# Masked attention taken through TensorE a unit of three steps at a time, with float32 scores

## The chip, the cores and the metric

One core of a Trainium2 chip. The metric is the device time of one execution in microseconds, as the median of several runs. The profile is of one execution on the same core.

## What is computed

Attention with a linear distance penalty, over 2 batches, 8 heads, 768 positions and 64 columns a head, then two feed-forward layers on 1536 tokens of 512 columns with 2048 hidden columns. A query sees the first 8 keys and its last 96 (both numbers are inputs):

```python
scores = scale * np.matmul(q, k.transpose(0, 1, 3, 2))
keep = is_global | is_local
scores = np.where(keep, scores + bias, -1000000000.0)
a = np.exp(scores - np.max(scores, axis=-1, keepdims=True))
a = a / (np.sum(a, axis=-1, keepdims=True) + 1e-09)
x = np.matmul(a, v)                       # then reshaped to (1536, 512)
h = x @ w_in;  x = (h / (1 + np.exp(-h))) @ w_out
h = x @ w_in2; out = (h * np.clip(h + 3, 0, 6) / 6) @ w_out2
```

q and k are float32 with values of about 0.66 in size; the weights come as float64 and are decoded on the chip.

## The kernel before, in words

**Units and steps.** The attention is cut into 16 units: a batch, a half of 384 positions, and a pair of heads. In the code they are counted from 0 with the pair running fastest, then the half, then the batch; units 0 to 3 and 8 to 11 have half 0. A unit has HB = 3 steps of 128 queries, so there are 48 steps. For a step, each of the two heads needs 256 keys: 128 of its own block and 128 made of 96 earlier ones and 32 global ones. The first step of a half 0 has 128 keys only.

**Stages of a step** (functions of these names, lines 321 to 440). `stage_a` brings a unit's keys and queries into transposed form: three TensorE transposes of keys and one of the earlier or global ones (psA), three of queries; ACT copies the result as a rounded high part (kh, qh, type float32r), DVE makes the remainder (kl, ql). `stage_b` makes scores as qh·kh + qh·kl + ql·kh, for both heads side by side in the 64-row halves of the array (psS, L388), then DVE adds the penalty and takes the extreme value (L394), then ACT takes the exponential and sums it (L398). `stage_b2` makes reciprocals of the sums on DVE (L404, L405) and scales z on POOL (L407). `stage_c` turns z by TensorE (psT, L416) and copies it out (pt: ACT for the first step of a unit, DVE for the others). `stage_d` multiplies with the values (psO, L435), both heads side by side in the 64-column halves of the array; after a unit's third step ACT copies the result as high part (xh, L439) and DVE makes the remainder (xl, L440).

**Order.** `attention_loop(n)` writes step n's scores, step n-1's scaling, step n-3's turn and step n-4's value products; `transposes(n)` adds a key part or a query part every third step each. `loop(n)` puts around it one piece of the feed-forward stage from `todo`, and the pieces of decoding weights and of gates from `late` and `slots`. The first pieces of the feed-forward layer are spread among the attention: from n = PRE = 16 one at every second step, 18 of them; after step 52 one at every step. An H piece is 12 matmuls (psH, L510), a Y piece 6 (psY, L683); in this first part of the stream they have 384 columns. During the attention all of them go through one PSUM bank, "f". Engines TensorE, ACT and POOL run in program order through the attention (`manual_schedule`); DVE and the SP queue are ordered by a scheduler at build time. At the start, before the loop, all are in program order.

**PSUM.** Eight banks in four rings: "S" 2 for scores (with "f" taking turns in the first 15 steps), "tr" 3 for transposes of any kind, "o" 2 for value products, "f" 1.

Of the kernel before, what the change touches and what calls it, by code (L numbers as in the profile page):

```python
# [18 lines left out]
P = 128  # L19
# [9 lines left out]
def attention_ffn_kernel(ctx, tc, q, k, v, n_global, n_local, w_in1, w_out1, w_in2, w_out2, out):  # L29
# [30 lines left out]
    ps_bufs = {"S": 2, "tr": 3, "o": 2, "f": 1}  # L60
# [136 lines left out]
    CL = 3  # L197
    LAG = CL + 1
    KOFF, QOFF, APOS, ATAG = 4, 3, 2, "tr"
    PRE = 3 * NP + LAG  # L200

# [17 lines left out]
    ZB = 4  # L219
# [42 lines left out]
    t1 = apool.tile([P, 2, W], F32, name="pat1", tag="z", bufs=ZB)  # L262
    t2 = apool.tile([P, 2, W], F32, name="pat2", tag="z", bufs=ZB)
# [57 lines left out]
    def stage_a(u, part):  # L321

        b, half, p = units[u]
        rk, kp, rq, rv, vp = raw[u]
        if part == 0:
            tr[u] = tuple(apool.tile([P, w], F32R, name=f"{n}{u}", tag=n) for n, w in (("kh", KW), ("kl", KW), ("qh", TB), ("ql", TB)))
        kh, kl, qh, ql = tr[u]
        ps = bank(ATAG, f"psA{u}_{part}")
# [26 lines left out]

        def glo(x):
            return x.unsqueeze(1).to_broadcast([P, HB - 1, G])


        parts = [(lambda x: tiles(x)[:, :, :P], own(ps[:, :TB])), (lambda x: tiles(x)[:, :HB - 1, P:], glo(ps[:, m - G:m]))]  # L360
        if half:
            parts.append((lambda x: x[:, :P], ps[:, TB:m]))

        def evac():
            for at_, src in parts:
                nc.scalar.copy(at_(kh), src)

        def rest():
            for at_, src in parts:
                nc.vector.tensor_tensor(out=at_(kl), in0=src, in1=at_(kh).bitcast(F32), op=ALU.subtract)  # L370

        return evac, rest

    zt, smt, ptt, pso = {}, {}, {}, {}

    def first(u, t):
        return units[u][1] == 0 and t == 0

    def stage_b(n, u, t):
        b, half, p = units[u]  # L380
        kh, kl, qh, ql = tr[u]
        tags = ("SS", "fS", "Sf")[n % 3] if n < PRE - 1 else "SS"
        ps = [bank(tags[h], f"psS{u}_{t}_{h}") for h in range(2)]
        o = P if first(u, t) else t * SP
        for i, (a, c) in enumerate(((qh, kh), (qh, kl), (ql, kh))):
            for h in range(2):
                hs = slice(h * D, (h + 1) * D)
                nc.tensor.matmul(ps[h][:, :W], a[hs, t * P:(t + 1) * P], c[hs, o:o + W], start=i == 0, stop=i == 2)  # L388
        w, nb = (P, nbs[p][0]) if first(u, t) else (W, nbs[p][1])
        z = apool.tile([P, 2, W], F32, name=f"z{u}_{t}", tag="z", bufs=ZB)  # L390
        mn = apool.tile([P, 2], F32, name=f"mn{u}_{t}", tag="mn", bufs=3)
        sm = apool.tile([P, 2], F32, name=f"sm{u}_{t}", tag="sm", bufs=3)
        for h in range(2):
            nc.vector.tensor_tensor_reduce(  # L394
                out=z[:, h, :w], in0=ps[h][:, :w], in1=nb[:, h, :], scale=1.0, scalar=3e38,
                op0=ALU.add, op1=ALU.min, accum_out=mn[:, h:h + 1])
        for h in range(2):
            nc.scalar.activation(out=z[:, h, :w], in_=z[:, h, :w], func=AF.Exp, bias=mn[:, h:h + 1], scale=-1.0,  # L398
                                 accum_out=sm[:, h:h + 1])
        zt[u, t], smt[u, t] = z, sm  # L400

    def stage_b2(u, t):
        z, sm, w = zt[u, t], smt.pop((u, t)), P if first(u, t) else W
        nc.vector.tensor_scalar(out=sm, in0=sm, scalar1=1e-9, scalar2=None, op0=ALU.add)  # L404
        nc.vector.reciprocal(sm, sm)  # L405
        for h in range(2):
            nc.gpsimd.tensor_scalar(out=z[:, h, :w], in0=z[:, h, :w], scalar1=sm[:, h:h + 1], scalar2=1.0,  # L407
                                    op0=ALU.mult, op1=ALU.mult)

    def stage_c(u, t):  # L410
        z = zt.pop((u, t))
        n = 1 if first(u, t) else 2
        ps = bank("tr", f"psT{u}_{t}").rearrange("p (h c q) -> p h c q", h=2, c=2)
        for h in range(2):
            for c in range(n):
                nc.tensor.transpose(ps[:, h, c, :], z[:, h, c * P:(c + 1) * P], ident)  # L416
        pt = apool.tile([P, 2, 2, P], F32, name=f"pt{u}_{t}", tag="pt")
        if t:
            nc.vector.tensor_copy(pt[:, :, :n, :], ps[:, :, :n, :])
        else:  # L420
            nc.scalar.copy(pt[:, :, :n, :], ps[:, :, :n, :])
        ptt[u, t] = pt

    def stage_d(u, t):
        b, half, p = units[u]
        rk, kp, rq, rv, vp = raw[u]
        pt = ptt.pop((u, t))
        if t == 0:
            pso[0] = bank("o", f"psO{u}")
        ps = pso[0]  # L430
        n = 1 if first(u, t) else 2
        for c in range(n):
            for h in range(2):
                lhs = (rv if c == n - 1 else vp)[:, h, t, :]
                nc.tensor.matmul(ps[h * D:(h + 1) * D, t * P:(t + 1) * P], lhs, pt[:, h, c, :], start=c == 0, stop=c == n - 1)  # L435
        if t == HB - 1:
            i = 2 * b + half
            hi, lo = (x[:, p, i * TB:(i + 1) * TB] for x in (xh, xl))
            nc.scalar.copy(hi, ps[:, :TB])  # L439
            return lambda: nc.vector.tensor_tensor(out=lo, in0=ps[:, :TB], in1=hi.bitcast(F32), op=ALU.subtract)  # L440

    seq = [(u, t) for u in range(len(units)) for t in range(HB)]
# [5 lines left out]
    def attention_loop(n):  # L448
        for f in queue.pop(n, []):
            f()  # L450
        if n < len(seq):
            u, t = seq[n]
            stage_b(n, u, t)
            if t == HB - 1 and u + 1 < NP:
                biases(u + 1)
        if n == 0:
            e, r = stage_a(1, 0)
            e()
            r()
            beyond()  # L460
        if 0 <= n - 1 < len(seq):
            stage_b2(*seq[n - 1])
        for f in rests.pop(n, []):
            f()
        if APOS == 0:
            transposes(n)
        if 0 <= n - CL < len(seq):
            stage_c(*seq[n - CL])
        if 0 <= n - LAG < len(seq):
            u, t = seq[n - LAG]  # L470
            f = stage_d(u, t)
            if f:
                at(n + 1, f)
                if u + 2 < len(units):
                    loads_v(u + 2)

        if APOS == 1:
            transposes(n)

    def transposes(n):  # L480
        for d, part in ((KOFF, 0), (QOFF, 1)):
            if (n + d) % HB == 0 and 1 <= (n + d) // HB < len(units):
                e, r = stage_a((n + d) // HB, part)
                e()
                rests.setdefault(n + 1, []).append(r)
                if part and (n + d) // HB + 2 < len(units):
                    loads((n + d) // HB + 2)

# [5 lines left out]
    def ffn_bank(kind, name):  # L494
        tags = ({"h": ("f",), "y": ("f",)}, {"h": ("f", "S"), "y": ("tr", "o")}, {"h": ("S",), "y": ("f", "o")})[ready[0]]
        ring = [t for t in tags[kind] if t in ps_bufs for _ in range(ps_bufs[t])]
# [265 lines left out]
    with tc.manual_schedule(engines=None):  # L762
        nc.vector.memset(three, 3.0)
        for i, ap in enumerate((n_global, n_local)):
# [21 lines left out]
    def loop(n):  # L786
# [5 lines left out]
        if APOS == 2:  # L792
            transposes(n)
# [271 lines left out]
```

## Time and profile before

| | us |
|---|---|
| median of 3 runs | 642.38 (640.3 to 645.43) |
| profiled execution, first to last instruction (span) | 638.6 |
| TensorE busy in the span | 617.2 |
| DVE / ACT / POOL busy | 489.9 / 417.4 / 161.0 |

The span is what the profile covers; the time of a run includes what lies before the first and after the last instruction. A second number of the profiled execution's own time is not in the profile, so the span stands for it. An engine's busy time counts stretches in which at least one of its instructions runs; matmuls overlap in the rows, so a row's duration is longer than its share of the engine.

### The profile page before, as it was taken

To read this page: it belongs to the slowest core of one execution; us is meant where nothing else is said; L and a number is where in the kernel's file an instruction comes from. 1 tells how busy PE (TensorE), PEld (TensorE's weight loads), DVE (VectorE), ACT (ScalarE), POOL (GpSimd) and SP (SyncE) were. 2 spreads that over 40 slices of the span, in tenths; PEclk is the share of its full clock that TensorE was granted. 3 is DMA by queue.
4 is the path that set the end of the run, shared out by engine and by line. 5 is a ranking of instruction groups with operands and counts; after the bars stand their busy time and mean duration, and the time that the engine had idled before them with its cause. 6 is when DMAs were issued, how large, how long until landed. Compare 5 with 4: busy or idle time off the path is not lost.

```text
span 638.6 us, 9729 instructions
## 1 busy us (share of the span) xinstructions
PE 617.2 (97%) x3214; PEld 498.9 (78%) x3214; DVE 489.9 (77%) x1107; ACT 417.4 (65%) x887; POOL 161.0 (25%) x233
## 2 busy tenths in 40 slices
PE   5889999999999999999999998999999999999996
PEld 3667777789888788888888887887788888888885
DVE  5899889953578796767675679988979696969453
ACT  4787877765557576666666676765766666666760
POOL 2776666561111111111212120011111111111110
PEclk9999999999999999999999999999999999999999
DMA  6555645349577667777776793186576868686544
GB/s 174 136 139 136 149 112 137 99 150 204 103 162 166 144 146 176 161 180 166 181 163 134 164 198 100 66 247 150 132 173 165 182 157 181 157 176 162 100 102 166
DMA packets 81625, 97.31 MB, mean 152 GB/s; under 512 B 55456, under 2 KB 55456, under 8 KB 81312
## 3 DMA queue, kind: packets, MB, share of 16 engines
q0 software_dynamic: 12576, 45.09, 37.7%
q1 hardware_dynamic: 68992, 51.53, 26.8%
q8 instruction: 27, 0.44, 0.3%
q14 instruction: 30, 0.25, 0.1%
HBM read 46.27 MB, written 3.15 MB: 77 GB/s over the span
## 4 chain that ended last, share of the span: by engine, by line
PE 35%; issue 25%; POOL 5%; DVE 2%; DMA 2%; ACT 1%; POOLq 0%; ACTq 0%; SPq 0%; DVEq 0%
PE psY L683 19%; PE psH L510 9%; POOL y L712 5%; PE psP_b L591 3%; PE psP_c L591 2%; PE psP_a L591 2%; DMA y<-st 1%; DMA raw<-in_moe_w_in_dram 1%; ACT st L708 0%; DVE g L541 0%; DVE da L1027 0%; DVE wol L148 0%; DVE dc L134 0%; DVE u L608 0%; ACT da L103 0%
## 5 line engine op out<-in xcount | busy, mean ns | idle before, releaser
L712 POOL DMA_DIRECT2D y<-st x78 | 66.9, 857 | 362.4 <-ACT st L708 357.2
L708 ACT COPY st<-psY 128x512 f32<-128x512 f32 x156 | 91.3, 586 | 51.6 <-PE psY L683 47.5
L510 PE MATMUL psH<-xh,wih 128*128 128x512 f32 (+1 forms) x216 | 83.2, 385 | 1.7 <-DVE g L541 1.7
L510 PE MATMUL psH<-xl,wih 128*128 128x512 f32 (+1 forms) x216 | 82.5, 382 | 0.0
L510 PE MATMUL psH<-xh,wil 128*128 128x512 f32 (+1 forms) x216 | 82.4, 382 | 0.0
L683 PE MATMUL psY<-gh,woh 128*128 128x512 f32 (+1 forms) x160 | 61.4, 384 | 0.0
L683 PE MATMUL psY<-gh,wol 128*128 128x512 f32 (+1 forms) x160 | 60.6, 378 | 0.0
L683 PE MATMUL psY<-gl,woh 128*128 128x512 f32 (+1 forms) x160 | 60.5, 378 | 0.0
L398 ACT ACTIVATE z<-z,mn 128x256 f32<-128x256 f32 (+1 forms) x96 | 46.5, 486 | 21.1 <-DVE mn L394 15.6
L407 POOL TENSOR_SCALAR z<-z,sm 128x256 f32<-128x256 f32 (+1 forms) x96 | 48.2, 514 | 43.9 <-DVE sm L405 18.4
L683 PE MATMUL psY<-woh,gl 128*128 128x512 f32 x144 | 56.1, 390 | 0.1
L683 PE MATMUL psY<-woh,gh 128*128 128x512 f32 x144 | 56.1, 390 | 0.1
L683 PE MATMUL psY<-wol,gh 128*128 128x512 f32 x144 | 56.0, 389 | 0.0
L510 PEld LDWEIGHTS psH<-xh,wih 128*128 128x128 f32 x216 | 40.5, 188 | 10.6 <-DVE g L541 2.1
L103 ACT ACTIVATE da<-raw 128x512 f32<-128x512 f32 x64 | 42.9, 670 | 5.9 <-DMA raw<-in_moe_w_in_dram 5.5
L510 PEld LDWEIGHTS psH<-xl,wih 128*128 128x128 f32 x216 | 40.5, 188 | 7.5 <-DVE xl L620 0.4
L510 PEld LDWEIGHTS psH<-xh,wil 128*128 128x128 f32 x216 | 40.5, 188 | 7.1
L1027 DVE SCALAR_TENSOR_TENSOR da<-raw,da 128x512 int32<-128x512 int32 x64 | 44.3, 693 | 1.2 <-DVE sm L404 0.2
L608 DVE TENSOR_TENSOR u<-psP_c,u 128x512 f32<-128x512 f32 x22 | 15.1, 688 | 34.5 <-ACT u L602 34.5
L532 ACT ACTIVATE a<-psH 128x512 f32<-128x512 f32 (+1 forms) x24 | 14.2, 590 | 40.4 <-PE psH L510 40.3
L551 DVE SCALAR_TENSOR_TENSOR gl<-a,gh 128x512 fp32r<-128x512 f32 (+1 forms) x34 | 23.2, 682 | 21.9 <-ACT gh L545 21.6
L1015 DVE TENSOR_SCALAR da<-da 128x512 f32<-128x512 f32 x64 | 28.3, 442 | 14.7 <-ACT da L103 14.7
(185 smaller groups left out, 1565.2 us busy)
## 6 DMA issues: line engine op xcount, KB each, us to landing
y<-st POOLq DMA_DIRECT2D x78, 512.0 KB, 4.8
raw<-in_moe_w_in_dram SPq DMA_DIRECT2D x32, 512.0 KB, 4.1
raw<-in_moe_w_out_dram SPq DMA_DIRECT2D x32, 512.0 KB, 3.3
rk<-in_k_dram SPq DMA_DIRECT2D x32, 96.0 KB, 2.5
rq<-in_q_dram SPq DMA_DIRECT2D x32, 96.0 KB, 2.9
rv<-in_v_dram SPq DMA_DIRECT2D x32, 96.0 KB, 2.6
out_dram<-y SPq DMA_DIRECT2D x12, 256.0 KB, 2.0
xf<-xh SPq DMA_DIRECT2D x2, 1024.0 KB, 6.7
```

Of the source, the lines that this page charges most:

```text
L103: nc.scalar.activation(out=t["a"], in_=raws[n][:, :, 1].bitcast(F32), func=AF.Abs)
L398: nc.scalar.activation(out=z[:, h, :w], in_=z[:, h, :w], func=AF.Exp, bias=mn[:, h:h + 1], scale=-1.0, accum_out=sm[:, h:h + 1])
L407: nc.gpsimd.tensor_scalar(out=z[:, h, :w], in0=z[:, h, :w], scalar1=sm[:, h:h + 1], scalar2=1.0, op0=ALU.mult, op1=ALU.mult)
L510: nc.tensor.matmul(ps, a[:, kt, js], x[:, kt, n0:n1], start=n == 0, stop=n == 3 * KT - 1)
L551: nc.vector.scalar_tensor_tensor(out=gl[:, j, :], in0=t["a"], scalar=2.0, in1=gh[:, j, :].bitcast(F32), op0=ALU.mult, op1=ALU.subtract)
L591: nc.tensor.matmul(ps, a[:, 2 * k + q, f * P:(f + 1) * P], x, start=p in (1, 5) and n == 0, stop=n == 5, skip_group_check=True)
L608: nc.vector.tensor_tensor(out=u, in0=st["c"], in1=u, op=ALU.add)
L683: nc.tensor.matmul(ps[:, :rhs.shape[1]], lhs, rhs, start=n == 0, stop=n == 3 * FC - 1)
L708: nc.scalar.copy(st[:, m % 2, :], part)
L712: late.setdefault(n, []).append(lambda: nc.gpsimd.dma_start(y, st, accum_op=ALU.add))
L1015: nc.vector.tensor_scalar(out=a, in0=a, scalar1=as_float(897 << 20), scalar2=as_float((1151 << 20) - 1), op0=ALU.max, op1=ALU.min)
L1027: nc.vector.scalar_tensor_tensor(out=ai, in0=w1, scalar=-0x40000000, in1=ai, op0=ALU.bitwise_and, op1=ALU.bitwise_or)
```

## The change

A unit goes through TensorE as a whole. `scores(u)` makes all three steps' scores at n = 3u with one float32 product per head and step, of unsplit queries and keys (kt, qt), into four banks: the two "S" banks hold steps 0 and 1 side by side, the two "o" banks hold step 2. The value products of unit u-2 follow at once, into a "tr" bank. The exponentials stay one step at a time. The sums of unit u-1 are turned into reciprocals once, at n = 3u, and all its z scaled then; its z is turned at n = 3u + 2, three blocks in a row. Key and query parts of unit u+1 stand at n = 3u and 3u + 1. `kl` and `ql` go away; DVE copies the global and earlier keys instead. z is held for two whole units (ZB = 2 of three steps each), pt in three buffers; ACT copies the middle step's pt, DVE the others. PRE becomes 17. Three products of zeros are put ahead of everything on TensorE. The rings of the feed-forward stage keep the same banks, the Y ring in another order.

```diff
-    KOFF, QOFF, APOS, ATAG = 4, 3, 2, "tr"
-    PRE = 3 * NP + LAG
+    LAG = 4
+    PRE = 3 * NP + LAG + 1
...
-    ZB = 4
+    ZB = 2
...
         if part == 0:
-            tr[u] = tuple(apool.tile([P, w], F32R, name=f"{n}{u}", tag=n) for n, w in (("kh", KW), ("kl", KW), ("qh", TB), ("ql", TB)))
+            tr[u] = tuple(apool.tile([P, w], F32, name=f"{n}{u}", tag=n) for n, w in (("kt", KW), ("qt", TB)))
...
         if part:
+            nc.scalar.mul(qt, ps[:, :TB], -1.0 / (D ** 0.5))
+            return
...
+        nc.scalar.copy(tiles(kt)[:, :, :P], own(ps[:, :TB]))
+        nc.vector.tensor_copy(tiles(kt)[:, :HB - 1, P:], glo(ps[:, m - G:m]))
         if half:
+            nc.vector.tensor_copy(kt[:, :P], ps[:, TB:m])
...
+    def scores(u):
+
+        kt, qt = tr[u]
+        two, one = ([bank(tag, f"psS{u}_{tag}{h}") for h in range(2)] for tag in "So")
+        place = {(h, t): one[h][:, :W] if t == 2 else two[h][:, t * W:(t + 1) * W] for h in range(2) for t in range(HB)}
+        for t in range(HB):
+            for h in range(2):
+                hs = slice(h * D, (h + 1) * D)
+                o = P if width(u, t) == P else t * SP
+                nc.tensor.matmul(place[h, t], qt[hs, t * P:(t + 1) * P], kt[hs, o:o + W], start=True, stop=True)
...
+    def normalise(u):
+        z, sm = zt[u], smt[u].rearrange("p t h -> p (t h)")
         nc.vector.tensor_scalar(out=sm, in0=sm, scalar1=1e-9, scalar2=None, op0=ALU.add)
         nc.vector.reciprocal(sm, sm)
+        for t in range(HB):
+            w = width(u, t)
+            for h in range(2):
+                nc.gpsimd.tensor_scalar(out=z[:, t, h, :w], in0=z[:, t, h, :w], scalar1=smt[u][:, t, h:h + 1], scalar2=1.0,
+                                        op0=ALU.mult, op1=ALU.mult)
+
+    def turn(u):
+        z = zt.pop(u)
+        for t in range(HB):
+            n = width(u, t) // P
+            ps = bank("tr", f"psT{u}_{t}").rearrange("p (h c q) -> p h c q", h=2, c=2)
+            for h in range(2):
+                for c in range(n):
+                    nc.tensor.transpose(ps[:, h, c, :], z[:, t, h, c * P:(c + 1) * P], ident)
+            pt = apool.tile([P, 2, 2, P], F32, name=f"pt{u}_{t}", tag="pt", bufs=3)
+            if t == 1:
+                nc.scalar.copy(pt[:, :, :n, :], ps[:, :, :n, :])
+            else:
+                nc.vector.tensor_copy(pt[:, :, :n, :], ps[:, :, :n, :])
+            ptt[u, t] = pt
+
+    def values(u):
...
+        ps = bank("tr", f"psO{u}")
...
+        nc.scalar.copy(hi, ps[:, :TB])
+        return lambda: nc.vector.tensor_tensor(out=lo, in0=ps[:, :TB], in1=hi.bitcast(F32), op=ALU.subtract)
...
     def attention_loop(n):
+        u, t = divmod(n, HB)
         for f in queue.pop(n, []):
             f()
+        if t == 0 and u < len(units):
+            scores(u)
+        if t == 0 and 0 <= u - 2 < len(units):
+            at(n + 1, values(u - 2))
+            if u < len(units):
+                loads_v(u)
+        if u < len(units):
+            exponentials(u, t)
             if t == HB - 1 and u + 1 < NP:
                 biases(u + 1)
         if n == 0:
             beyond()
+        if t == 0 and 0 <= u - 1 < len(units):
+            normalise(u - 1)
         for f in rests.pop(n, []):
             f()
+        if t < 2 and u + 1 < len(units):
+            stage_a(u + 1, t)
+            if t and u + 3 < len(units):
+                loads(u + 3)
+
+    def turns(n):
+        u, t = divmod(n, HB)
+        if t == 2 and 0 <= u - 1 < len(units):
+            turn(u - 1)
...
         nc.vector.memset(three, 3.0)
+        warm = fpool.tile([P, 512], F32, name="warm", tag="a")
+        nc.vector.memset(warm, 0.0)
+        for _ in range(3):
+            nc.tensor.matmul(bank("f", "psW"), warm[:, :P], warm, start=True, stop=True)
```

`exponentials(u, t)` holds the DVE and ACT instructions of `stage_b` unchanged for one step. In `loop(n)`, `turns(n)` stands after the feed-forward piece, where `transposes(n)` stood.

## Rows read from the trace of the kernel before

**Rows 1.** The page: span, and TensorE's busy time with its share.

```profile
span 638.6 us, 9729 instructions
...
PE 617.2 (97%) x3214; PEld 498.9 (78%) x3214; DVE 489.9 (77%) x1107; ACT 417.4 (65%) x887; POOL 161.0 (25%) x233
```

**Rows 2.** Busy us of each engine by stretch: PE, PEld, DVE, ACT, POOL, granted clock, DMA.

```profile
8.00:24.00 16.00, 13.85 (x78) 9.47 (x80) 11.71 (x52) 9.52 (x35) 7.39 (x19) 1.00 0.78 204
24.00:45.00 21.00, 17.91 (x165) 12.38 (x165) 20.13 (x77) 16.77 (x57) 16.36 (x27) 1.00 0.54 129
45.00:126.00 81.00, 79.50 (x678) 59.81 (x677) 74.37 (x272) 63.31 (x209) 53.49 (x80) 1.00 0.52 129
...
141.00:600.00 459.00, 456.00 (x2021) 377.68 (x2021) 352.63 (x628) 300.42 (x531) 69.39 (x80) 1.00 0.70 161
```

**Rows 3.** TensorE's timeline inside one unit: start, us, line, operands, count.

```profile
104.63 0.49 PE L331 MATMUL psA<-ident,rq 128*128 128x128 f32 x3
105.05 0.39 PE L388 MATMUL psS<-kh,qh 64*128 64x256 f32 x2
105.27 0.28 PE L388 MATMUL psS<-kl,qh 64*128 64x256 f32 x2
105.39 0.28 PE L388 MATMUL psS<-kh,ql 64*128 64x256 f32 x2
105.60 0.66 PE L416 MATMUL psT<-ident,z 128*128 128x128 f32 x4
106.18 0.44 PE L435 MATMUL psO<-pt,rv 128*64 128x128 f32 x4
...
107.70 0.44 PE L435 MATMUL psO<-pt,vp 128*64 128x128 f32 x4
...
108.28 0.45 PE L683 MATMUL psY<-gh,woh 128*128 128x384 f32 x1
108.57 0.34 PE L683 MATMUL psY<-gl,woh 128*128 128x384 f32 x1
108.74 0.33 PE L683 MATMUL psY<-gh,wol 128*128 128x384 f32 x1
```

**Rows 4.** Groups by line, 0 to 141 us: count, busy us, mean ns, idle before.

```profile
L407 POOL TENSOR_SCALAR z<-z,sm 128x256 f32<-128x256 f32 (+1 forms) x96 | 48.2, 514 | 43.9 <-DVE sm L405 18.4 <-ACT z L398 8.6 <-ACT kh L366 5.8
...
L419 DVE COPY pt<-psT 128x512 f32<-128x512 f32 x32 | 21.7, 678 | 0.8 <-PE psT L416 0.8
...
L404 DVE TENSOR_SCALAR sm<-sm 128x2 f32<-128x2 f32 x48 | 16.0, 333 | 3.8 <-ACT z L398 3.3
...
L370 DVE TENSOR_TENSOR kl<-psA,kh 128x384 fp32r<-128x384 f32 (+2 forms) x40 | 12.8, 359 | 0.7 <-ACT kh L366 0.7
...
L103 ACT ACTIVATE da<-raw 128x512 f32<-128x512 f32 x8 | 5.4, 679 | 0.0
```

**Rows 5.** ACT's timeline: two exponentials, and xh before the next copy.

```profile
103.31 0.52 ACT L398 ACTIVATE z<-z,mn 128x256 f32<-128x256 f32 x1
...
103.82 0.51 ACT L398 ACTIVATE z<-z,mn 128x256 f32<-128x256 f32 x1
...
104.56 0.49 ACT L439 CAST xh<-psO 128x384 fp32r<-128x384 f32 x1
104.93 0.50 ACT L697 COPY y<-psY 128x384 f32<-128x384 f32 x1
```

**Rows 6.** TensorE's timeline: first scores of units 0, 2, 15; first dense H piece.

```profile
8.09 0.58 PE L388 MATMUL psS<-kh,qh 64*128 64x256 f32 x2 [0.58 <-ACT qh L337]
...
23.86 0.39 PE L388 MATMUL psS<-kh,qh 64*128 64x256 f32 x2
...
126.49 0.39 PE L388 MATMUL psS<-kh,qh 64*128 64x256 f32 x2
...
140.78 0.44 PE L510 MATMUL psH<-xh,wih 128*128 128x384 f32 x1
```

**Rows 7.** TensorE's timeline at the start: the first three key turns.

```profile
5.56 0.87 PE L331 MATMUL psA<-ident,rk 128*128 128x128 f32 x3 [5.56 <-DMA rk<-in_k_dram]
```

More of the change, by code (lines that the diff above doesn't have):

```diff
@@ L368, in rest @@
[L368 to L385, printed above, removed]
+            nc.vector.tensor_copy(kt[:, :P], ps[:, TB:m])
@@ L386, in stage_b, with width @@
+    zt, mnt, smt, ptt, scored = {}, {}, {}, {}, {}
+    def width(u, t):
+        return P if units[u][1] == 0 and t == 0 else W
+    def scores(u):
+        kt, qt = tr[u]
+        two, one = ([bank(tag, f"psS{u}_{tag}{h}") for h in range(2)] for tag in "So")
+        place = {(h, t): one[h][:, :W] if t == 2 else two[h][:, t * W:(t + 1) * W] for h in range(2) for t in range(HB)}
+        for t in range(HB):
             for h in range(2):
                 hs = slice(h * D, (h + 1) * D)
-                nc.tensor.matmul(ps[h][:, :W], a[hs, t * P:(t + 1) * P], c[hs, o:o + W], start=i == 0, stop=i == 2)
@@ L389, in stage_b @@
[L389 to L392, printed above, removed]
+                o = P if width(u, t) == P else t * SP
+                nc.tensor.matmul(place[h, t], qt[hs, t * P:(t + 1) * P], kt[hs, o:o + W], start=True, stop=True)
+        scored[u] = place
+        zt[u] = apool.tile([P, HB, 2, W], F32, name=f"z{u}", tag="z", bufs=ZB)
@@ L397, in stage_b @@
         for h in range(2):
[L398 to L403, printed above, removed]
+            nc.scalar.activation(out=z[:, t, h, :w], in_=z[:, t, h, :w], func=AF.Exp, bias=mn[:, t, h:h + 1], scale=-1.0,
+                                 accum_out=sm[:, t, h:h + 1])
@@ L404, in stage_b2 @@
+    def normalise(u):
+        z, sm = zt[u], smt[u].rearrange("p t h -> p (t h)")
         nc.vector.tensor_scalar(out=sm, in0=sm, scalar1=1e-9, scalar2=None, op0=ALU.add)
         nc.vector.reciprocal(sm, sm)
[L406 to L422, printed above, removed]
@@ L425, in stage_d @@
+    def values(u):
         b, half, p = units[u]
         rk, kp, rq, rv, vp = raw[u]
[L427 to L440, printed above, removed]
@@ L442, in attention_ffn_kernel @@
-    seq = [(u, t) for u in range(len(units)) for t in range(HB)]
+        ps = bank("tr", f"psO{u}")
+        for t in range(HB):
+            pt = ptt.pop((u, t))
+            n = width(u, t) // P
+            for c in range(n):
+                for h in range(2):
+                    lhs = (rv if c == n - 1 else vp)[:, h, t, :]
+                    nc.tensor.matmul(ps[h * D:(h + 1) * D, t * P:(t + 1) * P], lhs, pt[:, h, c, :], start=c == 0, stop=c == n - 1)
+        i = 2 * b + half
+        hi, lo = (x[:, p, i * TB:(i + 1) * TB] for x in (xh, xl))
@@ L494, in ffn_bank @@
     def ffn_bank(kind, name):
[L495 to L496 removed]
+        ring = ({"h": ("f",), "y": ("f",)}, {"h": ("f", "S", "S"), "y": ("tr", "o", "tr", "o", "tr")}, {"h": ("S",), "y": ("f", "o", "o")})[ready[0]][kind]
         tag = ring[rot[kind] % len(ring)]
```

78 lines of the change are left out of this document (17 added, 61 removed).

## The prediction

> **What bounds the kernel now.** I read the page's first part, then the busy time by stretch, then TensorE's own timeline, then the groups by line. TensorE is busy for 617 of 638.6 us [rows 1]. By stretch [rows 2] there are three regimes: from 8 to 24 us it is busy 13.9 of 16; from 24 to 45 DVE is the full engine (20.1 of 21, TensorE 17.9); from 45 on TensorE is (79.5 of 81, then 456 of 459). So a microsecond taken from TensorE's attention work after 45 us should come off the end, if nothing else steps in, and after the attention nothing changes: the feed-forward stage takes the same products at TensorE's pace.
>
> What TensorE does in one attention step stands in [rows 3]. Split scores: three pairs of products (both heads at once, 0.12 us apart) take 0.55 us from 105.05 to 105.60, though 3 x 0.12 is 0.36. Four turns of z: 0.58. Value products, both column blocks: 0.58 (107.70 to 108.28). The feed-forward product after them shows why these sums are round: its first matmul takes 0.29 us to the next, the later ones 0.17. [...] I take 0.15 per change. Then a 128-column turn is (0.58 - 0.15)/4 = 0.108 us. A float32 value product has two records per head (x4 for two heads and one block), also 0.108 each, heads side by side.
>
> **The change, part by part.** Count units from 0 to 15; a unit whose half is 0 lacks a block in its first step.
>
> *TensorE.* Scores of a unit before: 3 x 0.55 = 1.66 us. After: one float32 product per step and head, two records of 256 columns, 2 x 0.108 = 0.215 each; if heads run side by side as both neighbours in [rows 3] do, 3 x 2 x 0.215 + 0.15 = 1.44. If not, 2.7. I take 1.44, since split scores in the same 64-row form and float32 value products both pair. Values: 3 x 0.58 = 1.74 becomes 6 x 0.215 + 0.15 = 1.44 (1.22 for half 0). Turns: 1.74 becomes 12 x 0.108 + 0.1 = 1.4 (1.2). Key and query turns keep their 0.11 each, 0.85 together. So attention costs TensorE about 5.1 us a unit (4.8 for half 0) against 6.1 (5.7): some 1 us, nearly all from fewer changes of form. The float32 pass itself costs more than the three split ones (0.43 against 0.36). If TensorE alone set the pace this were 16 us.
>
> *The others.* DVE loses kl (12.8 us) and ql and two thirds of the sums (16.0 us for 48 now) [rows 4], and gains small copies. That is worth time only between 24 and 45 us, and only until the next limit. POOL keeps its 96 scalings of 0.51 [rows 4]. ACT keeps its exponentials, loses 24 small key casts and gains larger z copies: about even.
>
> *The new wait.* What is late next is the order on ACT. At a unit's first step the program puts scores(u), then values(u-2) with their ACT copy xh, and only then the exponentials of u. ACT runs in that order, so it stands until TensorE has done scores and values: xh starts 1.44 + 1.44 + 0.1 = 3.0 us after scores(u) start. Queued behind it: two exponentials, the copy of kt, two exponentials, the copy of qt. Exponentials go at 0.51 us [rows 5], xh, kt and qt, all casts or copies of 384 columns, 0.37 apart as xh and its follower, with 0.5 until the last has landed [rows 5]: 0.37 + 1.02 + 0.36 + 1.02 + 0.5 = 3.3, so qt(u+1) is there at 6.3. Scores(u+1) need it. Before them in TensorE's order stands the third turn of u-1, which in a ring of three "tr" banks gets the bank of the query turn just copied: 0.1 + 0.43 + 0.1 more, 6.9 us from scores to scores (6.7 or 6.5 where halves 0 are involved). Without that bank it is 6.4. This exceeds TensorE's 5.1 wherever little feed-forward work falls. ACT work put into a first step lies on it too: decode pieces (0.68 long, some 0.6 apart) [rows 4], and gate casts and y copies of 384 columns (0.4 each, as xh).
>
> *Unit by unit.* A feed-forward piece stands at every odd step from 17: H pieces 12 x 0.175 = 2.1 us, Y pieces 6 x 0.175 + 0.1 = 1.15. The larger of TensorE's sum and the ACT loop:
> Units 2 to 4: 6.5 + 0.6, 6.5, 6.7 + 0.6 = 20.9.
> Units 5 to 9: 7.0 (TensorE, an H), 6.9 + 0.4 + 0.6, 7.2 (TensorE), 6.7 + 0.4, 6.7 + 0.6 = 36.5.
> Units 10 to 14: 6.9, 8.1 (TensorE, Y and H), 7.1, 8.2 (TensorE), 7.3 = 37.6.
> In all 95.0. Before, units 2 to 14 lasted from 23.86 to 126.49, 102.6 [rows 6]. Gain 7.6.
>
> *The first two units.* Scores of unit 0 start at 8.1 now and of unit 2 at 23.9 [rows 6]. [...] The three zero products of 512 columns, twice 0.43 us each by the record's pace above, last 2.6 us at full pace and 5.2 at half, from about 1.4 us: they lie beside the wait for data, and at half pace delay the key turns by at most 0.9. The new copy of the global keys stands ahead of the patterns on DVE and may push those from 4.7 to 7 us, so the first exponentials start near 10.4, as now. Units 0 and 1 have no values(u-2) to wait for. From 10.4: exponentials 0.8, key copy and decode 1.0, exponentials 1.0, query copy 0.5 put scores of unit 1 near 13.8; decode 0.6, exponentials 1.0, sums 0.4, six scalings 3.0 and the last turn 0.6 put unit 2 near 19.4. Gain 4.5; between 3 (half pace throughout) and 6 (patterns not held up).
>
> *The tail.* Before, unit 15 to the first dense H piece is 126.49 to 140.78, 14.3 [rows 6]. After, one more Y piece falls behind it: scores 1.44, the values of three units 4.3, the turns of two 2.8, an H piece 2.1, three Y pieces 3.5 make 14.2 of work; the last turns wait for exponentials and six scalings in a burst, and the last values for a z copy of 0.68 [rows 4]: 2 us. So 16.2. Loss 1.9.
>
> **Sum.** 7.6 + 4.5 - 1.9 = 10.2. The span of 638.6 becomes 628.4; the median of the runs, 642.4, lies 3.8 above the span, and that stays: 632.
>
> [...] TensorE still runs at half pace at 8.1 us (a pair of scores takes 0.58) and at full pace at 23.9 (0.39) [rows 6], though between them it is busy 13.9 of 16 us [rows 2]. [...]
>
> **Rivals.**
> 1. Heads not side by side in float32 scores. For: no 64-row float32 product in this trace. Against: both neighbours pair. Price: 1.3 us on the loop and on TensorE in each of 14 units, 1.3 in the tail: +20, 652. It decides from the point where scores of a unit exceed about 2.2 us (10 us over 14 units).
> 2. The clock falls back or never rises early. Unit 2 comes 1.5 us later and two to three units pay 1.44 + 1.1 more: +6, 638.
> 3. More waits in the loop: in-order DVE puts z copies (0.68) ahead of the reductions, or POOL's decode delays scalings. At 7.9 us a unit, the pace of before, units 2 to 14 give nothing: 640.
> 4. The query bank doesn't hold up the third turn: 0.55 less in nine loops, 627; with the loop gone and only TensorE's and ACT's own sums left (5.6 us a unit without feed-forward work, 84 for units 2 to 14) 622.
>
> **How the numbers follow.** Forecast 0.52 (626 to 638), rival 1 0.11, rivals 2 and 3 0.27, rival 4 0.10. One per cent, 6.4 us, is about what a measurement of this kernel can tell from none (its runs spread by 5). Faster than 636: most of the forecast and rival 4, 0.56; within: 0.33; slower: 0.11. The range 623 to 645 leaves out rival 1 and the extremes.
>
> **What would show it.** Right: scores of a unit take about 1.4 us in pairs; ACT idles before xh, released by psO, about 1 us a unit; TensorE idles before psT or psS released by ACT; unit 2 near 19.5, dense H pieces from about 130.5; from there the same length to the end. Wrong: score records one after another (rival 1); turns of 0.21 us after 10 us (2); TensorE without gaps from 45 us on (4); or a longer dense stage, which nothing here foresees.

## The result, and the profile after

| | before | after |
|---|---|---|
| median of the runs | 641.57 us (640.30 to 645.43, 4 runs) | 635.21 us (634.44 to 637.77, 4 runs) |
| after / before | | 0.990, 95% interval 0.987 to 0.993 |
| span of the profiled execution | 638.6 us | 632.8 us |

The changed kernel is 1% faster: 6.4 us by the medians, 5.8 by the spans. A second measurement gave 637.33 against 641.71, ratio 0.992 (0.989 to 0.994). The forecast was 632.0, with 10.2 us of gain in the span. The profiled run of the changed kernel took 634.86 us, 2.1 above its span.

The page of the changed kernel, lines that answer to [rows 1], with the granted clock in 40 slices:

```profile
span 632.8 us, 9365 instructions
...
PE 606.6 (96%) x3124; PEld 496.4 (78%) x3124; DVE 464.5 (73%) x1012; ACT 412.9 (65%) x863; POOL 160.4 (25%) x233
...
PEclk9998999999999999999999999999999999999998
```

TensorE is busy 10.6 us less, DVE 25 us less. The zeros are 5 us of TensorE's new time, but taking them out brings it down by only 1.2, to 605.4 (run 4): the first products then last longer, 24 of them from 4 to 12 us at 5.94 us of busy time, where 26 from 6.42 to 11 us take 3.84 behind the zeros. So on equal footing, without zeros in either kernel, TensorE saves 11.8 us and not the 16 that the prediction gave for TensorE alone. Of the 10.6 us, 5.8 came off the span; TensorE's idle time rose from 21.4 to 26.2. The 8 in the fourth slice is a loss of the clock that the kernel before didn't have. Busy time by stretch, the same windows as [rows 2]:

```profile
8.00:24.00 16.00, 12.01 (x86) 8.37 (x87) 12.82 (x63) 9.91 (x35) 8.41 (x21) 0.89 0.86 215
24.00:45.00 21.00, 15.98 (x149) 11.90 (x149) 17.62 (x65) 16.67 (x55) 14.45 (x25) 1.00 0.55 135
...
45.00:126.00 81.00, 74.25 (x629) 61.32 (x627) 58.17 (x218) 61.97 (x199) 56.32 (x86) 0.98 0.54 129
141.00:600.00 459.00, 456.26 (x2015) 377.01 (x2014) 353.32 (x629) 301.16 (x531) 66.25 (x78) 1.00 0.70 158
```

The dense stage is as it was (456.3 of 459 against 456.0). DVE is no longer the full engine from 24 to 45 us (17.6 of 21 against 20.1). From 45 to 126 us TensorE, full before at 79.5 of 81, now idles 6.75 us. Where the stages begin, from TensorE's timeline, answering to [rows 6, 7]:

```profile
1.50 5.08 PE L739 MATMUL psW<-warm 128*128 128x512 f32 x6 [1.50 <-DVE warm L737]
6.42 0.49 PE L329 MATMUL psA<-ident,rk 128*128 128x128 f32 x3
...
8.14 1.13 PE L369 MATMUL psS_S<-kt,qt 64*128 64x256 f32 x8 [0.58 <-DVE nval L278]
...
14.64 1.58 PE L369 MATMUL psS_S<-kt,qt 64*128 64x256 f32 x8 [3.81 <-ACT qt L331]
...
20.42 0.92 PE L369 MATMUL psS_S<-kt,qt 64*128 64x256 f32 x6
...
119.80 1.13 PE L369 MATMUL psS_S<-kt,qt 64*128 64x256 f32 x8
...
136.34 0.45 PE L482 MATMUL psH<-xh,wih 128*128 128x384 f32 x1
...
143.58 0.39 PE L482 MATMUL psH<-xh,wih 128*128 128x512 f32 x1
```

The last line is the first H piece of 512 columns. In the kernel before it is

```profile
149.23 0.39 PE L510 MATMUL psH<-xh,wih 128*128 128x512 f32 x1
```

So the parts that the prediction gave compare as follows:

| part | before | predicted | after | gain predicted | gain measured |
|---|---|---|---|---|---|
| scores of unit 2 start | 23.86 | 19.4 | 20.42 | 4.5 | 3.4 |
| units 2 to 14 | 102.6 | 95.0 | 99.4 | 7.6 | 3.2 |
| unit 15 to the first dense H piece | 14.3 | 16.2 | 16.5 | -1.9 | -2.2 |
| from there to the end | 497.9 | unchanged | 496.4 | 0 | 1.4 |

Most of the last row is work that changed sides. From the first dense H piece to the first H piece of 512 columns are 8.45 us before and 7.24 after: 24 products psY stand there before, 17 after. At 0.173 us from one to the next the seven make up the 1.21 us. They now stand ahead of the first dense H piece. Up to the first H piece of 512 columns both kernels have done 72 products psY, and from there to the end take 489.4 and 489.2 us.

The lengths of units 2 to 14, from first score to first score, against the prediction's:

| unit | 2 | 3 | 4 | 5 | 6 | 7 | 8 | 9 | 10 | 11 | 12 | 13 | 14 |
|---|---|---|---|---|---|---|---|---|---|---|---|---|---|
| predicted | 7.1 | 6.5 | 7.3 | 7.0 | 7.9 | 7.2 | 7.1 | 7.3 | 6.9 | 8.1 | 7.1 | 8.2 | 7.3 |
| after | 6.96 | 7.17 | 6.67 | **11.69** | 7.29 | 7.60 | 6.53 | 8.31 | 6.38 | 8.51 | 6.52 | 8.89 | 6.85 |

Twelve of the thirteen add up to 87.7 us against 88.0 predicted; there are misses of 0.4 to 1.0 either way in eleven of them, so that their sum agrees is in part luck. Unit 5 alone is 4.7 too long. TensorE's timeline there:

```profile
46.40 0.34 PE L482 MATMUL psH<-xl,wih 128*128 128x384 f32 x1
49.07 0.50 PE L482 MATMUL psH<-xh,wil 128*128 128x384 f32 x1 [2.34 <-POOL wil L148]
49.37 0.52 PE L482 MATMUL psH<-xh,wih 128*128 128x384 f32 x1
...
50.33 2.65 PE L403 MATMUL psT<-ident,z 128*128 128x128 f32 x12
52.91 0.92 PE L369 MATMUL psS_S<-kt,qt 64*128 64x256 f32 x6
```

and the instructions on ACT and POOL that bear on it:

```profile
43.09 0.64 ACT L145 CAST wih<-dc 128x512 fp32r<-128x512 f32 x1
...
45.03 2.76 POOL L393 TENSOR_SCALAR z<-z,sm 128x256 f32<-128x256 f32 x6 [3.93 <-PE psA L336]
47.75 1.27 POOL L148 TENSOR_TENSOR wil<-dc,wih 128x512 fp32r<-128x512 f32 x1
```

The H piece of step 17 is the first to use the second piece of decoded weights, and stops in the middle for its remainder `wil`. Dated from PRE, `wil` falls on step 15, where the program puts the six scalings of unit 4 ahead of it; in the kernel before it fell on step 14. POOL makes it only after them, and stood idle for 3.93 us before them, though the high part `wih` that the remainder is taken from was done at 43.73. Then a second cost: after the 2.34 us of waiting TensorE goes on at half pace (0.32 us from matmul to matmul instead of 0.17, twelve turns in 2.58 instead of 1.4 us); the records of the granted clock give half of the full level, 0.50, from 49.3 to 52.7 us.

Most of the rest behaves as foreseen. Unit 10 on TensorE:

```profile
82.64 1.13 PE L369 MATMUL psS_S<-kt,qt 64*128 64x256 f32 x8
83.61 0.60 PE L369 MATMUL psS_o<-kt,qt 64*128 64x256 f32 x4
84.14 0.44 PE L421 MATMUL psO<-pt,rv 128*64 128x128 f32 x4
...
85.38 0.55 PE L329 MATMUL psA<-ident,rk 128*128 128x128 f32 x3
...
88.47 0.63 PE L403 MATMUL psT<-ident,z 128*128 128x128 f32 x4 [0.17 <-DVE pt L408]
89.02 1.14 PE L369 MATMUL psS_S<-kt,qt 64*128 64x256 f32 x8
```

Twelve score records take 1.50 us (82.64 to 84.14): both heads side by side. On ACT, answering to [rows 5]:

```profile
85.50 0.48 ACT L424 CAST xh<-psO 128x384 fp32r<-128x384 f32 x1 [2.54 <-PE psO L421]
...
88.42 0.47 ACT L331 ACTIVATE qt<-psA 128x384 f32<-128x384 f32 x1
```

ACT stands before xh until the values are done; scores of unit 11 follow 0.13 us after the end of qt (88.89). That fits the predicted loop. The third turn (88.47), though, waits for DVE's pt and runs beside qt, not behind it; it ends when the scores start, so these rows alone don't say which of the two held them. Run 2 tests the order on ACT. The waits from 20 to 137 us, engine, instruction, releaser, total, times, longest:

```profile
ACT xh L424 <- PE psO L421: 24.6, 16, 3.1
...
POOL z L393 <- DVE sm L389: 16.2, 11, 3.9
...
PE psH L482 <- POOL wil L148: 2.3, 1, 2.3
```

And the groups that answer to [rows 4], up to 137 us:

```profile
L393 POOL TENSOR_SCALAR z<-z,sm 128x256 f32<-128x256 f32 (+1 forms) x96 | 45.9, 501 | 26.8 <-DVE sm L389 20.3 <-PE psA L336 3.9 <-PE psO L421 2.6
...
L388 DVE TENSOR_SCALAR sm<-sm 128x6 f32<-128x6 f32 x16 | 5.3, 328 | 0.6 <-ACT z L383 0.6
L351 DVE COPY kt<-psA 128x64 f32<-128x64 f32 x16 | 3.5, 219 | 8.8 <-ACT kt L350 8.8
```

The first instruction on the sums (L388) costs 5.3 us instead of 16.0, and 12.8 us of kl became 3.5 of this copy (and 2.2 of another one).

### The profile page after: what moved, and what is told of

Read it like the earlier page. It is cut to its first block, busy times and chain, and to the rows that moved or that the text cites. A ratio compares the mean times of both kernels' runs of the same rounds, so it can differ in the third digit from the quotient of the medians.

```text
span 632.8 us, 9365 instructions
## 1 busy us (share of the span) xinstructions
PE 606.6 (96%) x3124; PEld 496.4 (78%) x3124; DVE 464.5 (73%) x1012; ACT 412.9 (65%) x863; POOL 160.4 (25%) x233
## 4 chain that ended last, share of the span: by engine, by line
PE 58%; issue 23%; POOL 6%; DVE 5%; ACT 5%; DMA 2%; POOLq 0%; DVEq 0%; SPq 0%; ACTq 0%
PE psY L655 25%; PE psH L482 15%; POOL y L684 4%; PE psP_b L563 3%; PE psO L421 3%; PE psT L403 2%; PE psP_c L563 2%; PE psP_a L563 2%; PE psS_S L369 2%; ACT z L383 2%; DMA y<-st 1%; POOL z L393 1%; PE psW L739 1%; PE psS_o L369 1%; DVE z L379 1%
## 5 line engine op out<-in xcount | busy, mean ns | idle before, releaser
L684 POOL DMA_DIRECT2D y<-st x78 | 66.9, 857 | 364.3 <-ACT st L680 359.1
L393 POOL TENSOR_SCALAR z<-z,sm 128x256 f32<-128x256 f32 (+1 forms) x96 | 45.9, 501 | 26.8 <-DVE sm L389 20.3
L482 PEld LDWEIGHTS psH<-xh,wih 128*128 128x128 f32 x216 | 40.6, 188 | 10.6 <-DVE g L513 1.9
L986 DVE TENSOR_SCALAR da<-da 128x512 f32<-128x512 f32 x64 | 29.5, 461 | 15.9 <-ACT da L103 15.6
L523 DVE SCALAR_TENSOR_TENSOR gl<-a,gh 128x512 fp32r<-128x512 f32 (+1 forms) x34 | 23.1, 681 | 22.4 <-ACT gh L517 22.1
```

Of the source, the lines that this page charges most:

```text
L393: nc.gpsimd.tensor_scalar(out=z[:, t, h, :w], in0=z[:, t, h, :w], scalar1=smt[u][:, t, h:h + 1], scalar2=1.0, op0=ALU.mult, op1=ALU.mult)
L482: nc.tensor.matmul(ps, a[:, kt, js], x[:, kt, n0:n1], start=n == 0, stop=n == 3 * KT - 1)
L523: nc.vector.scalar_tensor_tensor(out=gl[:, j, :], in0=t["a"], scalar=2.0, in1=gh[:, j, :].bitcast(F32), op0=ALU.mult, op1=ALU.subtract)
L684: late.setdefault(n, []).append(lambda: nc.gpsimd.dma_start(y, st, accum_op=ALU.add))
L986: nc.vector.tensor_scalar(out=a, in0=a, scalar1=as_float(897 << 20), scalar2=as_float((1151 << 20) - 1), op0=ALU.max, op1=ALU.min)
```

## The experiments

Twelve kernels ran. The first four shared their runs of the kernel before (median 643.35), the next four too (641.7), and the last four (641.71).

**1. The decoding of that piece one step earlier** (12 steps ahead of step 17, so from step 5 as in the kernel before):

```diff
-        ahead = ((PRE, 11, 5, -1), (33, 27, 21, 15))[i][j] if i < 2 else (17, 13, 9, 5)[j] if chunks[i] == (1, 1) else ((20, 15, 11, 6), (18, 14, 9, 2))[fast(*chunks[i])][j]
+        ahead = ((PRE, 12, 5, -1), (33, 27, 21, 15))[i][j] if i < 2 else (17, 13, 9, 5)[j] if chunks[i] == (1, 1) else ((20, 15, 11, 6), (18, 14, 9, 2))[fast(*chunks[i])][j]
```

> The changed kernel with the second weight piece decoded one step earlier (its slots start at step 5 as before the change, not 6). Theory A (the 11.7 us of unit 5 come from the first H piece, which waits for wil on POOL behind the six scalings of unit 4, and from the half-rate clock that the gap brings): wil is made before that burst, unit 5 takes 7.0 to 7.5 us, no clock drop near 49 us, and the time falls by 4 us below the changed kernel's 635.2, to 631. Rival (the H piece waits anyway, for its values or for the burst itself): unit 5 stays at 10 us or more and the time within 1 us of 635.

Measured: 635.28 us (631.58 to 636.54), ratio 0.987 (0.984 to 0.991). Unit 5 fell from 11.69 to 8.34, without the wait for `wil` and without the half level at 49 us, but not to the 7.0 to 7.5 expected: TensorE now waits 0.60 and 0.18 us for copies of pt there. Yet the median was no better than the changed kernel's elsewhere. Its times fell into two groups, 631.6 to 632.5 and 635.2 to 636.5. Run again beside the changed kernel (runs 9 and 10) it was clearly faster.

**2. ACT's copy xh put behind the first two exponentials of the unit:**

```diff
-        nc.scalar.copy(hi, ps[:, :TB])
-        return lambda: nc.vector.tensor_tensor(out=lo, in0=ps[:, :TB], in1=hi.bitcast(F32), op=ALU.subtract)
+        return lambda: nc.scalar.copy(hi, ps[:, :TB]), lambda: nc.vector.tensor_tensor(out=lo, in0=ps[:, :TB], in1=hi.bitcast(F32), op=ALU.subtract)
...
-            at(n + 1, values(u - 2))
+            high, low = values(u - 2)
+            at(n + 1, low)
...
             exponentials(u, t)
+        if t == 0 and 0 <= u - 2 < len(units):
+            high()
+        if u < len(units):
...
```

> The changed kernel with ACT's copy xh of unit u-2 put behind the exponentials of unit u's first step, not ahead of them. Theory A (the order on ACT sets the pace of units without much feed-forward work): the wait of xh for psO on ACT (24.6 us in all in the changed kernel) mostly goes, units 2 to 4 fall from 6.9 to 6.0 or less, even units from 6 on from 6.7 to 6.2, and the time falls by 3 to 5 us, to 631. Rival (TensorE's own work or POOL's six scalings set the pace): the wait on ACT goes, the units keep their lengths and the time stays within 1 us of 635.

Measured: 630.26 us (629.82 to 631.27), ratio 0.980 (0.977 to 0.983). The waits from 20 to 137 us in this kernel:

```profile
ACT z L383 <- DVE mn L379: 10.3, 10, 1.8
...
ACT xh L424 <- PE psO L421: 3.9, 6, 1.5
```

ACT's wait for the values shrank from 24.6 to 3.9 us, units 2 to 14 from 99.4 to 93.5. So the order on ACT did set the pace. Of the 20.7 us of waiting taken away, 5.9 came off: ACT now waits 10.3 us for DVE's reductions instead, and unit 5 is still 10.24 long. TensorE's timeline there:

```profile
49.26 0.44 PE L485 MATMUL psH<-xh,wil 128*128 128x384 f32 x1 [2.38 <-POOL wil L148]
...
50.07 1.47 PE L403 MATMUL psT<-ident,z 128*128 128x128 f32 x12
```

The wait for `wil` is as long as in the changed kernel, but here the turns behind it go at full pace and no half level is recorded.

**3. Both edits together** (those of 1 and 2).

> Both edits together. If they act at different places: the sum of the two gains, 7 to 9 us below 635.2, so 626 to 628. If unit 5's wait for POOL takes back what the earlier units win: as the earlier decode alone, 631.

Measured: 629.25 us (627.07 to 632.12), ratio 0.979 (0.976 to 0.983); span 625.0, unit 5 at 8.70, units 2 to 14 in 92.1. It beats the changed kernel and the one before. Its advance on run 2 lies within the scatter of its runs, so neither of the two forecasts came true: the gains don't add up to 626 to 628, and it isn't held at 631 either.

**4. The changed kernel without the products of zeros:**

```diff
-        warm = fpool.tile([P, 512], F32, name="warm", tag="a")
-        nc.vector.memset(warm, 0.0)
-        for _ in range(3):
-            nc.tensor.matmul(bank("f", "psW"), warm[:, :P], warm, start=True, stop=True)
```

> The changed kernel without the three products of zeros. Theory A (the zeros raise the clock and so shorten the first units, at the price of key turns that start at 6.4 and not 5.6 us): key turns start at 5.6 but at half rate, unit 0 starts near 8, unit 2 comes 1 to 2 us later, units 2 and 3 may run at half rate and take 2 us more each: 1 to 5 us slower than 635.2. Rival (the waits on ACT cover the half rate): unit 2 within 0.5 us of 20.4 and the time within 1 us of 635, or 0.8 better.

Measured: 635.83 us (634.55 to 636.63), ratio 0.988 (0.985 to 0.991), as with them. Key turns start at 5.48 instead of 6.42 and unit 2 at 20.0 instead of 20.4. Without the zeros the records of the full clock begin at 12.4 us, not at 4.9, and the half level comes back from 26.1 to 29.5 instead of 15.2 to 18.6.

**5. The kernel before with float32 scores alone** (one product instead of three, no kl and ql; order, banks and sums as before):

```diff
-        for i, (a, c) in enumerate(((qh, kh), (qh, kl), (ql, kh))):
+        for i, (a, c) in enumerate(((qh, kh),)):
...
-                nc.tensor.matmul(ps[h][:, :W], a[hs, t * P:(t + 1) * P], c[hs, o:o + W], start=i == 0, stop=i == 2)
+                nc.tensor.matmul(ps[h][:, :W], a[hs, t * P:(t + 1) * P], c[hs, o:o + W], start=True, stop=True)
```

> The kernel before with float32 scores of unsplit queries and keys alone: kl and ql and two of the three products go, the order by single steps stays. Theory A (the gain comes from fewer changes of the array's form, the float32 product itself costs TensorE more): scores of a step take 0.63 us and not 0.55, DVE is relieved only where it set the pace (24 to 45 us), and the time is that of before or up to 4 us more, 642 to 647. Rival (dropping the split is the gain): 635 to 638, as the changed kernel.

Measured: 643.8 us, ratio 1.003 (1.0015 to 1.0045), slightly slower. TensorE's timeline of this kernel:

```profile
105.83 0.70 PE L388 MATMUL psS<-kh,qh 64*128 64x256 f32 x4
106.47 0.66 PE L416 MATMUL psT<-ident,z 128*128 128x128 f32 x4
```

Scores of a step take 0.64 us, against 0.55 for the three split products [rows 3]. Its units 2 and 3 are faster (6.54 and 6.11, before 7.01 and 6.94), where DVE was the bound; units 10 to 14 are slower (41.9 together, before 41.4), where TensorE was.

**6. The changed kernel with the split scores put back** (kl and ql on DVE, one buffer each; units, banks, sums and zeros as changed):

```diff
...
-            for h in range(2):
-                hs = slice(h * D, (h + 1) * D)
-                o = P if width(u, t) == P else t * SP
-                nc.tensor.matmul(place[h, t], qt[hs, t * P:(t + 1) * P], kt[hs, o:o + W], start=True, stop=True)
+            for i, (a, c) in enumerate(((qt, kt), (qt, kl), (ql, kt))):
+                for h in range(2):
+                    hs = slice(h * D, (h + 1) * D)
+                    o = P if width(u, t) == P else t * SP
+                    nc.tensor.matmul(place[h, t], a[hs, t * P:(t + 1) * P], c[hs, o:o + W], start=i == 0, stop=i == 2)
```

> The changed kernel with split scores (kt, kl, qt, ql and three products a step, kl and ql in one buffer each), all else as changed. Theory A (the order by units is the gain): scores of a unit take 1.3 us and not 1.5, ql adds 0.5 us behind qt on the way to the next scores, so 634 to 640, still faster than before. Rival (dropping the split is the gain): 641 or more.

Measured: 638.79 us, ratio 0.9955 (0.994 to 0.997). TensorE's timeline of this kernel:

```profile
62.04 0.63 PE L409 MATMUL psT<-ident,z 128*128 128x128 f32 x4 [1.20 <-DVE kl L358]
62.60 0.39 PE L375 MATMUL psS_S<-kt,qt 64*128 64x256 f32 x2
62.82 0.28 PE L375 MATMUL psS_S<-kl,qt 64*128 64x256 f32 x2
...
63.84 0.44 PE L427 MATMUL psO<-pt,vp 128*64 128x128 f32 x4
```

The nine pairs of split products of a unit take 1.24 us, less than the 1.50 of the float32 ones, and still the kernel is slower than the changed one: DVE's remainders stand in the loop, and turns wait for them 4.5 us in nine places. So the unit order with split scores is worth about 2.9 us, and dropping the remainders another 1.5 to 3.6 inside that order (against 637.33 of run 9 and 635.21), where in the old order it was worth less than nothing. How much of this is due to the single buffers of kl and ql was not tested.

**7. The kernel before with the products of zeros alone** (the four lines of run 4, added).

> The kernel before with the three products of zeros alone. Theory A (in the order by steps TensorE at half rate sets the pace of the first units, so here the zeros help, other than in the changed kernel): full rate from about 5 us, unit 2 starts 1 to 3 us earlier than 23.9 and the time is 1 to 3 us less than before. Rival (the clock is covered here too, or falls back at once): within 1 us of before.

Measured: 641.14 us, ratio 0.9997 (0.998 to 1.001). The records have the full clock from 6.4 us and half again from 16.7 to 20.1, where in the kernel before they begin at 20.2; unit 2 starts at 23.3 instead of 23.9, and nothing is left of it at the end.

**8. The changed kernel with a step's scores and an earlier unit's values taking turns on TensorE** (scores 0, values 0, scores 1, and so on: six runs of one form instead of two):

```diff
-        for t in range(HB):
+        def step(t):
...
+        return step
...
-    def values(u):
+    def values(u, step):
...
         for t in range(HB):
+            step(t)
             pt = ptt.pop((u, t))
...
-            scores(u)
+            step = scores(u)
+            if u < 2:
+                for j in range(HB):
+                    step(j)
...
-            at(n + 1, values(u - 2))
+            at(n + 1, values(u - 2, step if u < len(units) else lambda j: None))
```

> The changed kernel with scores and values of a unit alternating step by step (scores of step 0 of u, values of step 0 of u-2, and so on): the same products, four more changes of the array's form in each of units 2 to 15. Theory A (0.15 us per change, on the way to xh and to the next scores): 0.6 us more a unit, 8 us in all, 641 to 645. Rival (changes of form cost nothing where TensorE waits for ACT, or the earlier values win it back): within 2 us of 635.

Measured: 642.33 us, ratio 1.0001 (0.9986 to 1.0017): the whole gain is gone. TensorE's timeline of this kernel:

```profile
85.84 0.70 PE L369 MATMUL psS_S<-kt,qt 64*128 64x256 f32 x4
86.47 0.44 PE L423 MATMUL psO<-pt,rv 128*64 128x128 f32 x4
86.84 0.70 PE L369 MATMUL psS_S<-kt,qt 64*128 64x256 f32 x4
87.47 0.44 PE L423 MATMUL psO<-pt,vp 128*64 128x128 f32 x4
...
88.06 0.70 PE L369 MATMUL psS_o<-kt,qt 64*128 64x256 f32 x4
88.69 0.44 PE L423 MATMUL psO<-pt,vp 128*64 128x128 f32 x4
...
89.28 0.55 PE L329 MATMUL psA<-ident,rk 128*128 128x128 f32 x3
```

A step's scores take 0.63 us when alone, 0.50 when three stand together. From the first scores of unit 10 to the key turns is 3.44 us, against 2.74 in the changed kernel (82.64 to 85.38): 0.70 for four more changes of form, 0.175 per change. Units 6 to 14 add up to 72.9 us against 66.9, 0.66 more each.

**9. The changed kernel once more**, on one chip with the next three.

> The changed kernel itself, beside the next three on the same chip, so that their small differences can be read against it. Every theory: 635.2 us (634.4 to 637.8 so far), ratio to before 0.99; unit 5 again 11.7 us with a wait of 2.3 us for wil.

Measured: 637.33 us (635.42 to 637.97), ratio 0.992 (0.989 to 0.994); the same wait of 2.33 us for `wil`, unit 5 at 11.34.

**10. Run 1 again** (the same edit).

> The changed kernel with the second weight piece's decoding begun one step earlier, run once more beside the changed kernel. Theory A (unit 5 is long because the remainder wil stands behind the six scalings on POOL, and the 3.4 us it then lacks come off the end): 632 us, 3 below the changed kernel. Theory B (what unit 5 gains is given back before the dense stage, by a longer stretch at the half clock in the first 20 us and by other waits): within 1 us of the changed kernel, with 6.8 us at the half level before 20 us.

Measured: 632.59 us (632.11 to 634.76), ratio 0.9855 (0.983 to 0.988): 4.7 below the changed kernel beside it; unit 5 at 7.97. Its two runs above 634 include the profiled one, in which the half level is recorded twice, from 14.0 to 20.8 and from 27.6 to 34.5 us, and unit 2 starts at 22.1. All eleven runs of this edit have their median at 634.5, the ten of the changed kernel at 636.4. So the sign is settled. The size goes with the mean granted clock of an execution: the five of the eleven runs below 633 us have 0.992 to 0.995, the six above 634 have 0.988 to 0.990. In the profiled ones the difference is half clock in the first 35 us.

**11. Only the remainder of that piece moved from POOL to DVE:**

```diff
-            engine.tensor_tensor(out=t["l"], in0=t["c"], in1=t["h"].bitcast(F32), op=ALU.subtract)
+            (nc.vector if (i, j) == (0, 1) else engine).tensor_tensor(out=t["l"], in0=t["c"], in1=t["h"].bitcast(F32), op=ALU.subtract)
```

> The changed kernel with only one instruction moved: the remainder wil of the second weight piece is made by DVE instead of POOL, so that it no longer stands behind the six scalings of unit 4. Theory A (POOL's order is the cause): the H piece of unit 5 waits less than 0.5 us for wil, TensorE doesn't fall to the half level at 49 us, unit 5 takes about 8.5 us instead of 11.7, and the time is some 2 to 3 us shorter, 632 to 633. Rival (the piece is late all along, whatever engine makes the remainder): the wait stays near 2 us and unit 5 above 11.

Measured: 632.07 us (631.91 to 633.45), ratio 0.985 (0.982 to 0.987), 5.3 below the changed kernel beside it. TensorE's timeline at the same place:

```profile
46.64 0.43 PE L482 MATMUL psH<-xh,wih 128*128 128x384 f32 x1
...
48.64 0.33 PE L482 MATMUL psH<-xh,wil 128*128 128x384 f32 x1
48.82 1.47 PE L403 MATMUL psT<-ident,z 128*128 128x128 f32 x12
50.22 1.14 PE L369 MATMUL psS_S<-kt,qt 64*128 64x256 f32 x8
```

The H piece runs through, the turns follow at full pace, and unit 5 lasts 7.44 us. Only one instruction went to another engine, so its place on POOL was the cause.

**12. The earlier decoding without the zeros** (the edits of 1 and 4).

> The changed kernel with the earlier decoding and without the three zero products. If the stretch at the half clock before 20 us comes from the zero products (the granted clock rises with them and falls again in the thin work behind them), no half level is recorded between 12 and 20 us, and the time is that of the earlier decoding less some 2 us. If the zeros bring nothing, as without the earlier decoding, it is within 1 us of it.

Measured: 633.23 us (632.12 to 634.35), ratio 0.986 (0.984 to 0.989), as run 10 within the scatter. No half level is recorded from 17.5 to 27.7 us, but there is one from 27.7 to 31.1. The zeros change where TensorE runs at half pace and bring no time.

## Why the prediction was right, and where its sum was off

The direction was right and so was the mechanism: the changes of form saved on TensorE, and ACT's order as the next limit. The measured gain, 5.8 of 10.2 us in the span, falls short by 4.4. Unit 5 lacks 4.7 and the start 1.1; the other units, the tail and the dense stage together give 1.4 back.

- *Scores side by side.* Right: 1.50 us a unit, 1.44 forecast. The first rival (2.7 us) falls. That the float32 pass costs TensorE more than the split one was right too (0.64 us a step against 0.55), and run 5 shows that it gains nothing by itself. The 0.15 us a change of the array's form were an estimate between the 0.19 and the 0.12 left over in [rows 3] (0.55 less 3 x 0.12, 0.29 less 0.17), and no row shows a change by itself; run 8 gives 0.175. What takes the time in a change isn't shown.
- *TensorE alone.* The 16 us don't follow from the prediction's own terms: 1.66, 1.74, 1.74 and 0.85 are 5.99 us a unit before, not 6.1, which against 5.1 makes some 14. Without zeros 11.8 were measured, with stretches at half pace among them.
- *ACT's new wait.* Right in place, too small in size: forecast about 1 us a unit, measured 24.6 in 16. Run 2 takes most of it away and gains 5.9 us in units 2 to 14. The longer wait did not lengthen the loop: in unit 10 xh starts 2.86 us after the scores, where 3.0 was forecast.
- *The third turn in the query's bank.* Wrong as a wait on the path: the step "gets the bank of the query turn just copied: 0.1 + 0.43 + 0.1 more, 6.9 us" doesn't show. Units 10 and 12 last 6.38 and 6.52 against 6.9 and 7.1, close to the 6.4 given for a loop without that bank, so the fourth rival held in the shorter units. The longer ones made up for it: units 9, 11 and 13 lie 0.4 to 1.0 above their forecast, with waits that the sum had not priced (in unit 9 a turn waits 0.81 for DVE's copy L351, in unit 11 an H piece 0.24 for ACT's copy of y, both at feed-forward steps). That the total came out is luck.
- *Unit 5: the step that failed.* The prediction gave it "7.0 (TensorE, an H)" and counted a later PRE only as a shift of the feed-forward pieces. It did not follow the decoding, which is placed relative to PRE, nor POOL's queue, in which the six scalings that now come in a burst stand ahead of a remainder that the next H piece needs. The third rival had POOL's decode delay the scalings; what came was the reverse. Measured 11.69; with the remainder taken off POOL (run 11) 7.44. Of the 4.25 between them 2.34 is the wait; the rest is mostly what TensorE then does at half pace (the turns alone 1.2, four matmuls 0.6). That half pace isn't bound to the wait: run 2 has the wait without it, and unit 5 there lasts 10.24.
- *The first two units.* 3.4 of 4.5. Unit 1 started at 14.64, 0.8 later than forecast, still at the full level; TensorE had stood 3.81 us before it. The clock then fell at 15.2 us, and the scores of unit 1 took 2.4 us (to the next turns at 17.01) instead of 1.5. So the clock did fall back, as the second rival had it, but unit 2 came only 1.0 us late, and the later units did not pay for it. By that rival's own terms its price was 6.6 to 9.1 us, not 6. The zeros took 5.08 us, near the 5.2 given for half pace, and three key turns behind them 0.49 us, against 0.87 in [rows 7]. They changed only where TensorE runs at half pace, not the time (runs 4, 7 and 12: 635.83 against 635.21 us, 641.14 against 641.7, 633.23 against 632.59). Each fall that was looked at has waits on TensorE shortly ahead of it: 3.81 us ahead of the one at 15.2 us and 2.34 ahead of 49.3 in the changed kernel, 1.01 and 0.61 ahead of 26.1 in run 4, 1.69 and 0.61 ahead of 27.7 in run 12. What makes the clock rise or fall no run shows.
- *The tail and the dense stage.* The tail's size was right, 16.5 against 16.2, its parts less so: 25 products psY stand in it, where three pieces, 18 products, were counted, and 12 before. That the rest would be unchanged was wrong in the sum: the prediction charged the tail for one more Y piece and didn't take it off what follows. Seven of those products, 1.2 us, are missing behind the first dense H piece, most of the 1.4 us by which that part is shorter. From the first H piece of 512 columns on, the two kernels differ by 0.2 us, less than profiles of one kernel's variants do among themselves (488.6 to 490.6 us for the changed kernel and its variants).
- *The median.* A run's time lies 2.0 to 2.2 us above its span in the changed kernel and 1.7 to 1.9 in the kernel before, where both are given. So about 1.8 of the 3.8 that the prediction put between span and median is this distance. The other 2 came from the profiled execution of before being quicker than its median, as, by less, that of the changed kernel was too (634.86 against 635.21).

## What to carry to other kernels

When work is gathered into bursts, list on every in-order engine what now stands behind the burst and who needs it soonest: here one 1.27 us instruction behind six scalings on POOL cost some 4 us in its unit, where the whole change brought 6. A constant that dates other pieces (PRE) must be followed through everything computed from it. And after an engine's load is cut, look for the instruction that waits longest in program order on the next one: moving a single ACT copy behind the exponentials brought 5 us more.

## What the runs showed of the hardware that was not expected

A wait on TensorE can cost more than its length, but needn't. Behind 2.34 us without `wil` the granted clock read the half level, 0.50, for 3.4 us, although TensorE was busy again; so it did in runs 4 and 9, behind 2.38 and 2.33 us (in run 4 its mean from 45 to 60 us was 0.89, in run 9 the twelve turns took 2.74 us). In run 2, behind 2.38 us at the same place, it stayed at the full level, and the twelve turns took 1.47 us. What decides isn't shown. In the kernel before the records read the full level from 20.2 us to the last microsecond without a break.

Raising the clock early did not keep it up. With the zeros it is full from 4.9 us (6.8 in run 9), and half again from 15.2 to 18.6 (13.7 to 20.5): 3.4 us at the half level in one execution of the changed kernel and 6.8 in the other. The spans of run 1's edit go with such stretches: its profiled executions had 6.8 us at that level ahead of 35 us (span 630.4) and 13.6 (span 632.7).
